# Attention outputs of one pair issued together with the state update and scores of the next, PSUM banks divided anew

## The chip, the cores and the metric

The kernel runs on one core of a Trainium2 chip. The metric is the device time of one execution in microseconds, the median of several runs. A profiled execution shows each engine: TensorE (PE, with its weight loads as PEld), VectorE (DVE), ScalarE (ACT), GpSimd (POOL) and SyncE (SP), which issues the transfers.

## The reference

A linear attention with decay feeds two gated layers over 3072 tokens (B=4, S=768, H=8 heads of D=48; 384 columns).

```python
for t in range(S):
    cur = einsum('bhd,bhe->bhde', u * k[t], v[t])
    y[t] = einsum('bhd,bhde->bhe', r[t], state + cur)
    state = w[t][..., None] * state + einsum('bhd,bhe->bhde', k[t], v[t])
x = y as (3072, 384)
x = ((x @ w_a) * (x @ w_b)) @ w_out          # d_ff 1536
out = square(maximum(x @ w_in, 0)) @ w_out2  # d_ff 2048
```

## The kernel before

**Attention.** The recurrence is taken in chunks of 64 tokens, two chunks at a time: a *pair* p is 128 tokens of one batch for all eight heads, and there are 24 pairs, six to a batch. For a pair, DVE scans the decays (`at_scan`, line 246) and takes reciprocals (`at_recip`, four calls, line 250); POOL scales keys and receptances into the tiles `rk` and `ar` (`at_kr`, `at_rr`) and builds the diagonal term (`at_u1`, `at_diag`). TensorE then has four groups of plain float32 matmuls:

- `at_B` (line 295) transposes the scaled keys into tile `kt`, copied by ACT to `kn` (`at_B2`);
- `at_C` (line 304) makes the state update `ds`, 16 matmuls (8 for the last pair of a batch); DVE adds it to the state `vs` (`at_C2`, four instructions, lines 319 to 323);
- `at_A` (line 281) makes the scores `sc`, 32 small matmuls; DVE copies them under a mask into `ar` (`at_A2`, line 293);
- `at_D` (line 325) makes the outputs `yp`, 32 small matmuls from `ar` and `vs`; ACT copies them to `ys` (`at_D2`), and two transfers store them (`at_store`).

**Layers.** Stage one works in seven blocks of tokens (`BLOCKS1`: 384, 256, 384, then four of 512), stage two in six of 512. Weights come as 64-bit words and are decoded on chip into a high and a low float32r part (`dec_*`, lines 181 to 208: sign, shift, add, high, low, mostly on DVE and ACT); the twelve units of stage one are decoded while the first block runs. A step f of stage one has two products `ua` and `ub` (`prod`, line 350: nine matmuls each into a PSUM tile `pa`), a copy of the first by ACT (line 364), the multiply g on DVE that reads the second (`mult`, line 368), a split of g into `gh` (ACT) and `gl` (POOL), and nine matmuls into three accumulators `acc` (`down`, line 381) some steps later. Stage two has one product a step. The x of a block is loaded from what the attention stored and split by ACT and DVE (`xh`, `xl`).

**PSUM.** There are eight banks: three for `pa` (pool `ps_ab`), three for `acc`, two for the attention's four tiles in turn (pool `ps_at`).

**What sets the order.** Nothing is scheduled on the chip: a planner (class `Plan`, line 47) is run when the program is built. `plan_pair` (line 443) and `plan_step` (line 544) register operations with a cost for each engine, a due time (from the table `KNOB`), what they depend on, and which ring of buffers they take (`acq`) and give back (`rel`). The planner always starts the ready operation with the earliest due time on a free engine, and the order so found is the order in which instructions are issued on each engine. The rings of the plan (line 426) have the numbers of the pools. An engine works strictly in this order: an instruction that waits holds up all behind it.

Of the kernel before, what the change touches and what calls it, by code (L numbers as in the profile page):

```python
# [15 lines left out]
PSUM = bass.MemoryType.PSUM  # L16
DRAM = bass.MemoryType.DRAM

B, H, S, D = 4, 8, 768, 48
NT, DM = B * S, H * D  # L20
F1, F2 = 1536, 2048
C = 64
NP = NT // 128
# [10 lines left out]
EN = HE + HC  # L34
WS = 256.0

KNOB = dict(START=12.39, FIRST=8.84, LEAD=11.15, DEC=4.0, DO=13.13, XO=5.05, X2=-28.46, D2=35.09, LW=13.05, LT=16.03,
            LV=-5.89, LV2=3.32, LN=0.14, scan=2.4, rec=7.4, kr=0.01, rr=-1.74, u1=-0.02, u2=-0.72, dg=-10.16,
            gd=-17.94, A=-4.1, B=9.68, C=-0.57, D=11.41, T2=4.18, EARLY=2.03, WAIT=0)
ENG = dict(kr=("POOL",), da=("DVE", "POOL"), dl=("DVE", "POOL"), rr=("POOL", "DVE"), u2=("DVE",), xs=("DVE",), d2=("ACT",),  # L40
           b2=("ACT",), gl=("POOL",), gh=("ACT",))
SAFE = 2.0 ** 90
FLOOR = 2.0 ** -50
EV, OD = slice(C, C + D), slice(0, D)
# [78 lines left out]
def fused_kernel(ctx, tc, tpk, natpk, vpk, v2pk, upk, cst, w1pk, w2pk, out):  # L123
# [5 lines left out]
    op = ctx.enter_context(tc.tile_pool(name="op", bufs=2))  # L129
    ap = ctx.enter_context(tc.tile_pool(name="ap", bufs=2))  # L130
    dp = ctx.enter_context(tc.tile_pool(name="dp", bufs=1, space=DRAM))
    ps_ab = ctx.enter_context(tc.tile_pool(name="ps_ab", bufs=3, space=PSUM))
    ps_acc = ctx.enter_context(tc.tile_pool(name="ps_acc", bufs=1, space=PSUM))
    ps_at = ctx.enter_context(tc.tile_pool(name="ps_at", bufs=2, space=PSUM))

    ident = const.tile([128, 128], F32, name="ident")
    floor = const.tile([128, HE], F32, name="floor")
# [143 lines left out]
    def at_A(p):  # L281
        t, ar = RK[p], AR[p % 2]
        P = PS[p, "A"] = ps_at.tile([128, HC], F32, tag="at", name="sc")
        for h in range(H):
            ks = slice(TK + h * C, TK + (h + 1) * C)
            cs = slice(h * C, (h + 1) * C)
            nc.tensor.matmul(out=P[0:C, cs], lhsT=t[EV, ks], rhs=ar[EV, 0, cs], start=True, stop=True)  # L287
            nc.tensor.matmul(out=P[C:128, cs], lhsT=t[OD, ks], rhs=ar[OD, 1, cs], start=True, stop=True)
# [36 lines left out]
    def at_D(p):  # L325
        ar, vs = AR[p % 2], VS[p % 2]
        P = PS[p, "D"] = ps_at.tile([112, HC], F32, tag="at", name="yp")
        for h in range(H):
            cs = slice(h * C, (h + 1) * C)
            es = slice(h * D, (h + 1) * D)  # L330
            nc.tensor.matmul(out=P[OD, cs], lhsT=vs[0:112, 0, es], rhs=ar[0:112, 0, cs], start=True, stop=True)  # L331
            nc.tensor.matmul(out=P[EV, cs], lhsT=vs[:, 1, es], rhs=ar[:, 1, cs], start=True, stop=True)  # L332
# [102 lines left out]
    tau = [K["START"]]
# [7 lines left out]
    def plan_pair(p):  # L443
        j, i = place[p]
        m = BLOCKS1[j] // 128
        cold = 1.9 if p <= BLOCKS1[0] // 128 else 1.0
# [5 lines left out]
        def add(name, engs, prio, fn, deps=(), **kw):  # L452
            plan.add((name, p), engs, q - prio, fn, deps, **kw)
# [15 lines left out]
        for k in range(2):  # L469
# [3 lines left out]
            rel=[("nat", p)])  # L473
        add("gd", {"ACT": 1.27}, K["gd"], lambda e: at_guard(p),
            [(("rr", 0), p), (("rr", 1), p), ("A", p), ("B", p), *((("rec", k), p) for k in range(4))], rel=[("rk", p)])
        add("A", {"PE": 1.28 * cold}, K["A"], lambda e: at_A(p), [("kr", p), (("rr", 0), p), (("rr", 1), p)],
            acq=[("at", (p, "A"))])
        add("A2", {"DVE": 1.48}, K["A"], lambda e: at_A2(p), [("A", p), (("dg", 0), p), (("dg", 1), p), "consts"],
            rel=[("at", (p, "A")), ("dg", p)])
        add("B", {"PE": 0.41 * cold}, K["B"], lambda e: at_B(p), [("kr", p), "consts"], acq=[("at", (p, "B"))])  # L480
        add("B2", both(0, 448, *ENG["b2"]), K["B"], lambda e: at_B2(p, e), [("B", p)], acq=[("ky", (p, "k"))],
            rel=[("at", (p, "B"))])
        add("C", {"PE": 1.0 * cold}, K["C"], lambda e: at_C(p), [("B2", p), ("LV2", p), ("D", p - 1)], acq=[("at", (p, "C"))],
            rel=[("ky", (p, "k"))])
        add("C2", {"DVE": 2.35 if p % PPB != PPB - 1 else 1.2}, K["C"], lambda e: at_C2(p), [("C", p), ("C2", p - 1), ("D", p - 1)],
            rel=[("at", (p, "C"))])
        add("D", {"PE": 1.23 * cold}, K["D"], lambda e: at_D(p), [("A2", p), ("C2", p), ("LV", p), ("gd", p)],
            acq=[("at", (p, "D"))], rel=[("ef", p)])
        add(("D2", 0), both(0, HC, *ENG["d2"]), K["D"], lambda e: at_D2(p, 0, e), [("D", p)], acq=[("ky", (p, "y"))])
        add(("D2", 1), both(0, HC, *ENG["d2"]), K["D"], lambda e: (at_D2(p, 1, e), PS.pop((p, "D"))),  # L490
            [("D", p), (("D2", 0), p)], rel=[("at", (p, "D"))])
        for c in range(2):
            add(("ST", c), {"DMA": 0.6}, K["D"], lambda e, c=c: at_store(p, c), [(("D2", c), p), (("ST", c - 1), p)],
                rel=[("ky", (p, "y"))] if c else [], lat=DMA_LAT)
# [118 lines left out]
    for p in range(NP):  # L613
        plan_pair(p)
# [225 lines left out]
```

## Time and profile before

| what | us |
|---|---|
| median of 3 runs | 1009.81 (1009.52 to 1010.01) |
| the profiled execution's own time | 1009.95 |
| its span | 1008.1 |
| TensorE busy in the span | 950.3 (94%) |
| DVE busy | 488.0 (48%) |
| POOL busy | 457.3 (45%) |
| ACT busy | 385.2 (38%) |

The span runs from the first to the last instruction of the program; the execution's own time has 1.85 us more around it. Matmuls overlap in the array, so the time that counts for TensorE is not the length of an instruction but the step from one start to the next.

### The profile page before, as it was taken

The numbers are of one execution on the slowest core, as the hardware profiler recorded it, in microseconds if no ns is written. First come the engines' busy times: TensorE is split into PE (matmuls) and PEld (weight loads), VectorE is DVE, ScalarE is ACT, GpSimd is POOL, SyncE is SP. The second block draws the span as 40 slices with busy tenths as digits, with TensorE's granted clock in tenths as the row PEclk, the third lists the DMA queues.
The fourth block names the chain that finished last, engine by engine and source line by source line (L and its number), as shares of the span: only waits on it lengthen the run. The fifth ranks groups of instructions, "written<-read, shape, count | busy, mean of one in ns | idle before, by whom it ended". The sixth has DMA issues, their size and how long they took to land.

```text
span 1008.1 us, 15015 instructions
## 1 busy us (share of the span) xinstructions
PE 950.3 (94%) x5982; PEld 803.7 (80%) x5982; DVE 488.0 (48%) x585; ACT 385.2 (38%) x591; POOL 457.3 (45%) x359
## 2 busy tenths in 40 slices
PE   3558799999999999999999999999999999999997
PEld 2448699999978787888788888888888888888885
DVE  7799976786564554554222578821121221211111
ACT  1566534333332333233232567433342332422332
POOL 6645478786655455564212254433333233333332
PEclk9969899999999999999999999999999999999999
DMA  9995235544433433332011555010010000100001
GB/s 255 313 315 157 59 96 141 163 121 130 121 86 91 107 106 104 104 92 81 9 40 63 173 196 195 1 53 11 1 64 0 32 32 1 63 1 1 32 0 36
DMA packets 57791, 91.89 MB, mean 91 GB/s; under 512 B 23664, under 2 KB 31600, under 8 KB 57712
## 3 DMA queue, kind: packets, MB, share of 16 engines
q1 hardware_dynamic: 57712, 90.84, 29.7%
q8 instruction: 49, 0.80, 0.3%
q14 instruction: 30, 0.25, 0.1%
HBM read 76.66 MB, written 14.16 MB: 90 GB/s over the span
## 4 chain that ended last, share of the span: by engine, by line
PE 87%; DVE 4%; DMA 3%; issue 2%; ACT 2%; POOL 1%; SPq 0%; DVEq 0%; ACTq 0%; POOLq 0%
PE pa L357 16%; PE pa L358 16%; PE pa L359 15%; PE acc L384 12%; PE acc L386 11%; PE acc L385 11%; PE sc L287 2%; PE yp L331 2%; PE ds L310 2%; DVE z L194 1%; DMA rk<-in_tpk_dram 1%; PE kt L298 1%; DMA vs<-in_vpk_dram 1%; DMA raw<-in_w1pk_dram 1%; DVE raw L190 1%
## 5 line engine op out<-in xcount | busy, mean ns | idle before, releaser
L378 POOL TENSOR_TENSOR gl<-a,gh 128x512 fp32r<-128x512 f32 (+2 forms) x180 | 238.7, 1327 | 445.4 <-ACT gh L175 444.3
L359 PE MATMUL pa<-xh,w 128*128 128x512 f32 (+2 forms) x792 | 295.3, 373 | 5.0 <-DVE w L208 5.0
L358 PE MATMUL pa<-xl,w 128*128 128x512 f32 (+2 forms) x792 | 295.1, 373 | 4.3 <-DVE xl L535 4.3
L357 PE MATMUL pa<-xh,w 128*128 128x512 f32 (+2 forms) x792 | 297.0, 375 | 0.6 <-ACT w L175 0.4
L364 ACT ACTIVATE a<-pa 128x512 f32<-128x512 f32 (+2 forms) x180 | 102.4, 569 | 291.0 <-PE pa L359 239.1
L384 PE MATMUL acc<-gh,w 128*128 128x512 f32 (+2 forms) x540 | 208.7, 386 | 0.0
L386 PE MATMUL acc<-gl,w 128*128 128x512 f32 (+2 forms) x540 | 202.6, 375 | 0.1
L385 PE MATMUL acc<-gh,w 128*128 128x512 f32 (+2 forms) x540 | 202.6, 375 | 0.0
L175 ACT ACTIVATE gh<-a 128x512 fp32r<-128x512 f32 (+2 forms) x180 | 108.3, 602 | 227.2 <-DVE a L368 179.7
L368 DVE TENSOR_TENSOR a<-a 128x512 f32<-128x512 f32 x96 | 67.9, 707 | 253.2 <-ACT a L364 253.2
L359 PEld LDWEIGHTS pa<-xh,w 128*128 128x128 f32 x792 | 150.5, 190 | 29.0 <-DVE w L208 6.2
L358 PEld LDWEIGHTS pa<-xl,w 128*128 128x128 f32 x792 | 150.8, 190 | 27.4 <-DVE xl L535 4.9
L357 PEld LDWEIGHTS pa<-xh,w 128*128 128x128 f32 x792 | 150.6, 190 | 25.1 <-ACT w L175 1.2
L368 DVE TENSOR_TENSOR a<-a,pa 128x512 f32<-128x512 f32 (+2 forms) x84 | 50.8, 606 | 174.9 <-PE pa L359 173.0
L384 PEld LDWEIGHTS acc<-gh,w 128*128 128x128 f32 x540 | 101.5, 188 | 19.7
L386 PEld LDWEIGHTS acc<-gl,w 128*128 128x128 f32 x540 | 101.5, 188 | 17.4 <-POOL gl L378 0.4
L385 PEld LDWEIGHTS acc<-gh,w 128*128 128x128 f32 x540 | 101.6, 188 | 15.3
L252 DVE RECIPROCAL ef<-ef 112x128 f32<-112x128 f32 x96 | 83.3, 916 | 0.4
L277 POOL TENSOR_TENSOR ar<-ident,dg 64x512 f32<-64x512 f32 x48 | 56.1, 1169 | 38.3 <-PE yp L332 23.9
L260 POOL TENSOR_TENSOR ar<-rk,ef 48x512 f32<-48x512 f32 (+1 forms) x48 | 64.7, 1349 | 17.0 <-DVE ef L247 7.4
L247 DVE TENSOR_TENSOR_SCAN ef<-ef,floor 112x520 f32<-112x520 f32 x24 | 38.4, 1603 | 5.0 <-DMA ef<-in_tpk_dram 4.9
L331 PE MATMUL yp<-ar,vs 112*48 112x64 f32 x384 | 30.0, 237 | 10.3 <-issue 9.0
(54 smaller groups left out, 850.6 us busy)
## 6 DMA issues: line engine op xcount, KB each, us to landing
raw<-in_w1pk_dram SPq DMA_DIRECT2D x36, 384.0 KB, 5.7
raw<-in_w2pk_dram SPq DMA_DIRECT2D x32, 384.0 KB, 3.8
rk<-in_tpk_dram SPq DMA_DIRECT2D x24, 448.0 KB, 4.2
v<-in_v2pk_dram SPq DMA_DIRECT2D x24, 384.0 KB, 3.2
nat<-in_natpk_dram SPq DMA_DIRECT2D x24, 384.0 KB, 4.2
ef<-in_tpk_dram SPq DMA_DIRECT2D x24, 227.5 KB, 4.1
vs<-in_vpk_dram SPq DMA_DIRECT2D x48, 96.0 KB, 3.3
xd<-ys SPq DMA_DIRECT2D x48, 96.0 KB, 3.1
```

The source lines that it names most:

```text
L175: nc.scalar.activation(out=out, in_=in_, func=ACTF.Copy, **({} if scale is None else {"scale": scale}))
L252: nc.vector.reciprocal(out=hv(inv(p), C)[:, h0:h0 + 2], in_=hv(ext(p), C + 1)[:, h0:h0 + 2, 1:])
L260: eng(e).tensor_tensor(out=hv(AR[p % 2][rows, c, :], C), in0=hv(RK[p][rows, TR:TK], C), in1=hv(ext(p), C + 1)[rows, :, 0:C], op=ALU.mult)
L357: nc.tensor.matmul(out=out, lhsT=blk(wh, k), rhs=h, start=(k == 0), stop=False)
L358: nc.tensor.matmul(out=out, lhsT=blk(wh, k), rhs=l, start=False, stop=False)
L359: nc.tensor.matmul(out=out, lhsT=blk(wl, k), rhs=h, start=False, stop=(k == KD - 1))
L364: nc.scalar.activation(out=a[:, 0:n], in_=P[:, 0:n], func=func, scale=scale)
L368: eng(e).tensor_tensor(out=a[:, 0:n], in0=a[:, 0:n], in1=b[:, 0:n], op=ALU.mult)
L378: eng(e).tensor_tensor(out=gl[:, 0:n], in0=g[:, 0:n], in1=gh[:, 0:n], op=ALU.subtract)
L384: nc.tensor.matmul(out=o, lhsT=blk(wh, d), rhs=gh[:, 0:n], start=first, stop=False)
L385: nc.tensor.matmul(out=o, lhsT=blk(wl, d), rhs=gh[:, 0:n], start=False, stop=False)
L386: nc.tensor.matmul(out=o, lhsT=blk(wh, d), rhs=gl[:, 0:n], start=False, stop=last)
```

## The change

From the ninth pair on (p >= `ALONE`, which is 8), the outputs of pair p-1, the state update of pair p and its scores are one operation of the planner: `at_D(p - 1)`, `at_C(p)` and `at_A(p)` are issued back to back on TensorE, when all that the three depend on is there. Pair 8 has its update and scores together, and the last pair its outputs alone. The transposes `at_B` stay an operation of their own. The pool `ps_ab` goes from three banks to two and `ps_at` from two to three, and the plan's rings with them. All numbers of `KNOB` but two are new, so that the planner's order changes on every engine, from the start on.

```diff
-KNOB = dict(START=12.39, FIRST=8.84, LEAD=11.15, DEC=4.0, DO=13.13, XO=5.05, X2=-28.46, ...
+KNOB = dict(START=13.52, FIRST=7.12, LEAD=18.8, DEC=4.0, DO=13.32, XO=5.1, X2=-14.73, ...
...
+ALONE = 8
...
-    ps_ab = ctx.enter_context(tc.tile_pool(name="ps_ab", bufs=3, space=PSUM))
+    ps_ab = ctx.enter_context(tc.tile_pool(name="ps_ab", bufs=2, space=PSUM))
...
-    ps_at = ctx.enter_context(tc.tile_pool(name="ps_at", bufs=2, space=PSUM))
+    ps_at = ctx.enter_context(tc.tile_pool(name="ps_at", bufs=3, space=PSUM))
...
-    plan = Plan(dict(ef=3, rk=2, nat=2, dg=2, ky=3, at=2, ab=3, a=3, gg=3, o=2, x=2, z=2), KNOB["WAIT"])
+    plan = Plan(dict(ef=3, rk=2, nat=2, dg=2, ky=3, at=3, ab=2, a=3, gg=3, o=2, x=2, z=2), KNOB["WAIT"])
...
-        add("A", {"PE": 1.28 * cold}, K["A"], lambda e: at_A(p), [("kr", p), (("rr", 0), p), (("rr", 1), p)],
-            acq=[("at", (p, "A"))])
+        alone = p < ALONE
+        depA, acqA = [("kr", p), (("rr", 0), p), (("rr", 1), p)], [("at", (p, "A"))]
+        depC, acqC = [("B2", p), ("LV2", p), ("D", p - 1)], [("at", (p, "C"))]
+        depD, acqD = [("A2", p), ("C2", p), ("LV", p), ("gd", p)], [("at", (p, "D"))]
+        if alone:
+            add("A", {"PE": 1.28 * cold}, K["A"], lambda e: at_A(p), depA, acq=acqA)
+            add("C", {"PE": 1.0 * cold}, K["C"], lambda e: at_C(p), depC, acq=acqC, rel=[("ky", (p, "k"))])
+        elif p == ALONE:
+            add("A", {"PE": 1.9}, K["A"], lambda e: (at_C(p), at_A(p)), [*depA, *depC], acq=[*acqC, *acqA],
+                rel=[("ky", (p, "k"))])
+        else:
+            add("A", {"PE": 2.85}, K["A"], lambda e: (at_D(p - 1), at_C(p), at_A(p)),
+                [*depA, *(x for x in depC if x[0] != "D"), ("A2", p - 1), ("C2", p - 1), ("LV", p - 1), ("gd", p - 1)],
+                acq=[("at", (p - 1, "D")), *acqC, *acqA],
+                rel=[("ky", (p, "k")), ("ef", p - 1)])
...
+        if alone or p == NP - 1:
+            add("D", {"PE": 1.23 * cold}, K["D"], lambda e: at_D(p), depD, acq=acqD, rel=[("ef", p)])
```

TensorE in the steady part, blocks of 512 tokens, before (names of tiles as above; each pair of rows that alternates is shown once):

```order
L386 MATMUL acc_2932<-gl,w_554 128x512
L310 MATMUL ds<-v_93,kn 48x96
L312 MATMUL ds<-v_93,kn 48x96
...
L384 MATMUL acc_2957<-gh,w_554 128x512
...
L359 MATMUL pa<-xh,w_763 128x512
L287 MATMUL sc<-ar_89,rk 64x64
L288 MATMUL sc<-ar_89,rk 64x64
...
L384 MATMUL acc_2932<-gh,w_638 128x512
```

and with the change, at the same place:

```order
L387 MATMUL acc_3702<-gl,w_487 128x512
L332 MATMUL yp<-ar_90,vs_92 48x64
L333 MATMUL yp<-ar_90,vs_92 48x64
...
L311 MATMUL ds<-v_93,kn 48x96
L313 MATMUL ds<-v_93,kn 48x96
...
L288 MATMUL sc<-ar_89,rk 64x64
L289 MATMUL sc<-ar_89,rk 64x64
...
L385 MATMUL acc_3714<-gh,w_487 128x512
```

Update and scores stood apart with acc and pa matmuls between them, and the outputs further on; now outputs (of the other `ar` and `vs` buffer, so of the pair before), update and scores follow each other. After the first block of stage one, TensorE goes from pa or acc matmuls to such groups (kt alone not counted) 52 times before and 23 times now, 15 of them for all three at once.

DVE at the end of the first block, before (L199 and L208 decode weights, L368 is g, L247 the scan, L252 the reciprocals, L293 the masked copy):

```order
L368 TENSOR_TENSOR a<-a,pa 128x384
L199 ISA z<-raw_623,z 128x2304
L293 COPY_PREDICATED ar_89<-mask,sc 64x512 x2
L368 TENSOR_TENSOR a<-a,pa 128x384
L247 SCALAR_TENSOR_TENSOR ef<-ef,floor 112x520
L252 RECIPROCAL ef<-ef 112x128 x4
L273 TENSOR_REDUCE dg<-nat 128x8
L368 TENSOR_TENSOR a<-a,pa 128x384
```

and with the change:

```order
L369 TENSOR_TENSOR a<-a,pa 128x384
L209 TENSOR_TENSOR w_1038<-z,w_1038 128x1152
L200 ISA z<-raw_644,z 128x2304
L369 TENSOR_TENSOR a<-a,pa 128x384
L248 SCALAR_TENSOR_TENSOR ef<-ef,floor 112x520
L209 TENSOR_TENSOR w_1080<-z,w_1080 128x1152
L253 RECIPROCAL ef<-ef 112x128 x4
L369 TENSOR_TENSOR a<-a,pa 128x384 x2
```

The g rows in the first fence are the tenth, eleventh and twelfth of the block; in the second they are the ninth, the tenth, and the eleventh and twelfth together, with the scan and the reciprocals ahead of both.

DVE in the steady part with the change, one pair's time:

```order
L274 TENSOR_REDUCE dg<-nat 128x8
L369 TENSOR_TENSOR a<-a,pa 128x512
L248 SCALAR_TENSOR_TENSOR ef<-ef,floor 112x520
L253 RECIPROCAL ef<-ef 112x128 x4
L369 TENSOR_TENSOR a<-a,pa 128x512 x2
L294 COPY_PREDICATED ar_89<-mask,sc 64x512 x2
L320 TENSOR_TENSOR ds<-ds,vs_91 48x384
```

Before, a g stood between the scan and the reciprocals, and the four state instructions between the first two reciprocals and the last two; now the scan and all four reciprocals stand between one g and the next.

## Rows read from the trace of the kernel before

**Rows 1.** The page: busy time by engine; a DMA issue, with KB and us to landing.

```profile
PE 950.3 (94%) x5982; PEld 803.7 (80%) x5982; DVE 488.0 (48%) x585; ACT 385.2 (38%) x591; POOL 457.3 (45%) x359
...
xd<-ys SPq DMA_DIRECT2D x48, 96.0 KB, 3.1
```

**Rows 2.** Busy time by stretch: start:end, us, engines' busy (x instructions), PE clock, DMA.

```profile
66.40:145.50 79.10, 68.55 (x442) 64.80 (x442) 71.84 (x66) 42.64 (x56) 45.11 (x28) 0.91 0.40 126
145.50:198.00 52.50, 52.49 (x617) 50.25 (x612) 41.23 (x61) 21.01 (x45) 42.33 (x41) 1.00 0.55 154
198.00:517.00 319.00, 318.82 (x2458) 266.01 (x2457) 166.77 (x226) 102.12 (x177) 173.68 (x144) 1.00 0.34 94
```

**Rows 3.** TensorE's waits, 146 us to the end: us in total, times, longest.

```profile
PE yp L332 <- DVE ar L293: 0.2, 1, 0.2
```

**Rows 4.** Instructions in time, TensorE, 322 to 332 us: start us, us, what.

```profile
322.90 0.39 PE L385 MATMUL acc<-gh,w 128*128 128x512 f32 x1
323.12 0.39 PE L386 MATMUL acc<-gl,w 128*128 128x512 f32 x1
323.44 0.28 PE L310 MATMUL ds<-v,kn 128*48 128x96 f32 x1
...
324.24 0.50 PE L384 MATMUL acc<-gh,w 128*128 128x512 f32 x1
324.58 0.40 PE L385 MATMUL acc<-gh,w 128*128 128x512 f32 x1
...
329.58 0.39 PE L359 MATMUL pa<-xh,w 128*128 128x512 f32 x1
329.90 0.27 PE L287 MATMUL sc<-ar,rk 48*64 48x64 f32 x1
...
330.98 0.50 PE L384 MATMUL acc<-gh,w 128*128 128x512 f32 x1
```

**Rows 5.** Instructions in time, TensorE, 205 to 208 us.

```profile
205.40 0.34 PE L359 MATMUL pa<-xh,w 128*128 128x384 f32 x1
205.66 0.28 PE L310 MATMUL ds<-v,kn 128*48 128x96 f32 x1
...
206.46 0.27 PE L287 MATMUL sc<-ar,rk 48*64 48x64 f32 x1
...
207.54 0.45 PE L357 MATMUL pa<-xh,w 128*128 128x384 f32 x1
207.82 0.34 PE L358 MATMUL pa<-xl,w 128*128 128x384 f32 x1
```

**Rows 6.** Instructions in time, DVE, first 150 us; in brackets idle time and releaser.

```profile
32.38 0.58 DVE L319 TENSOR_TENSOR ds<-ds,vs 48x384 f32<-48x384 f32 x1 [5.43 <-PE ds L312]
...
132.20 0.55 DVE L368 TENSOR_TENSOR a<-a,pa 128x384 f32<-128x384 f32 x1 [0.19 <-ACT a L364]
132.67 2.95 DVE L247 TENSOR_TENSOR_SCAN ef<-ef,floor 112x520 f32<-112x520 f32 x1
135.65 3.39 DVE L252 RECIPROCAL ef<-ef 112x128 f32<-112x128 f32 x4
```

**Rows 7.** Groups by line, DVE, 0 to 145.5 us: busy us, mean ns | idle before.

```profile
L252 DVE RECIPROCAL ef<-ef 112x128 f32<-112x128 f32 x24 | 20.4, 908 | 0.1
...
L247 DVE TENSOR_TENSOR_SCAN ef<-ef,floor 112x520 f32<-112x520 f32 x6 | 10.3, 1739 | 2.2 <-DMA ef<-in_tpk_dram 2.2
```

**Rows 8.** Instructions in time, TensorE, 138 to 146 us.

```profile
138.35 0.33 PE L384 MATMUL acc<-gh,w 128*128 128x384 f32 x1
...
142.51 0.55 PE L298 MATMUL kt<-ident,rk 112*128 112x112 f32 x4
143.69 0.86 PE L310 MATMUL ds<-v,kn 128*48 128x96 f32 x8 [0.63 <-ACT kn L175]
...
145.56 0.39 PE L357 MATMUL pa<-xh,w 128*128 128x256 f32 x1
```

**Rows 9.** Instructions in time, DVE, 315 us.

```profile
315.71 0.69 DVE L368 TENSOR_TENSOR a<-a,pa 128x512 f32<-128x512 f32 x1 [4.87 <-PE pa L359]
```

More of the change, by code (lines that the diff above doesn't have):

```diff
@@ L35 @@
 WS = 256.0
-KNOB = dict(START=12.39, FIRST=8.84, LEAD=11.15, DEC=4.0, DO=13.13, XO=5.05, X2=-28.46, D2=35.09, LW=13.05, LT=16.03,
-            LV=-5.89, LV2=3.32, LN=0.14, scan=2.4, rec=7.4, kr=0.01, rr=-1.74, u1=-0.02, u2=-0.72, dg=-10.16,
-            gd=-17.94, A=-4.1, B=9.68, C=-0.57, D=11.41, T2=4.18, EARLY=2.03, WAIT=0)
+KNOB = dict(START=13.52, FIRST=7.12, LEAD=18.8, DEC=4.0, DO=13.32, XO=5.1, X2=-14.73, D2=33.64, LW=15.56, LT=19.97,
+            LV=-2.26, LV2=-0.35, LN=7.51, scan=2.25, rec=6.21, kr=-1.09, rr=5.02, u1=-0.24, u2=2.9, dg=-11.72,
+            gd=-27.44, A=-3.1, B=4.87, C=-16.56, D=10.05, T2=4.14, EARLY=2.77, WAIT=0)
 ENG = dict(kr=("POOL",), da=("DVE", "POOL"), dl=("DVE", "POOL"), rr=("POOL", "DVE"), u2=("DVE",), xs=("DVE",), d2=("ACT",),
            b2=("ACT",), gl=("POOL",), gh=("ACT",))
+ALONE = 8
 SAFE = 2.0 ** 90
@@ L475, in plan_pair @@
             [(("rr", 0), p), (("rr", 1), p), ("A", p), ("B", p), *((("rec", k), p) for k in range(4))], rel=[("rk", p)])
-        add("A", {"PE": 1.28 * cold}, K["A"], lambda e: at_A(p), [("kr", p), (("rr", 0), p), (("rr", 1), p)],
-            acq=[("at", (p, "A"))])
+        alone = p < ALONE
[13 more added lines that the diff above has]
+                rel=[("ky", (p, "k")), ("ef", p - 1)])
+        if not alone:
+            plan.index["C", p] = plan.index["A", p]
+            if p > ALONE:
+                plan.index["D", p - 1] = plan.index["A", p]
+        if alone or p == NP - 1:
+            add("D", {"PE": 1.23 * cold}, K["D"], lambda e: at_D(p), depD, acq=acqD, rel=[("ef", p)])
         add("A2", {"DVE": 1.48}, K["A"], lambda e: at_A2(p), [("A", p), (("dg", 0), p), (("dg", 1), p), "consts"],
@@ L482, in plan_pair @@
             rel=[("at", (p, "B"))])
-        add("C", {"PE": 1.0 * cold}, K["C"], lambda e: at_C(p), [("B2", p), ("LV2", p), ("D", p - 1)], acq=[("at", (p, "C"))],
-            rel=[("ky", (p, "k"))])
         add("C2", {"DVE": 2.35 if p % PPB != PPB - 1 else 1.2}, K["C"], lambda e: at_C2(p), [("C", p), ("C2", p - 1), ("D", p - 1)],
             rel=[("at", (p, "C"))])
-        add("D", {"PE": 1.23 * cold}, K["D"], lambda e: at_D(p), [("A2", p), ("C2", p), ("LV", p), ("gd", p)],
-            acq=[("at", (p, "D"))], rel=[("ef", p)])
         add(("D2", 0), both(0, HC, *ENG["d2"]), K["D"], lambda e: at_D2(p, 0, e), [("D", p)], acq=[("ky", (p, "y"))])
```

## The prediction

> **What bounds the kernel now.** I read the page's busy table first. TensorE is busy for 94% of the span of 1008.1 us; the next engine, VectorE, for 48% [rows 1]. A share over the whole span hides stages, so the second view is the table by stretches [rows 2]. From 66.4 to 145.5 us TensorE works 68.55 of 79.10 us at a granted clock of 0.91, while DVE works 71.84: this stretch is the first block of stage one, and in it DVE, which decodes the weights and runs the attention's vector steps, is the bound. From 145.5 us on TensorE is busy for all of each stretch, at clock 1.00. The third view is the list of TensorE's waits from 146 us to the end: it holds a single wait of 0.2 us [rows 3]. So after 145.5 us only one thing can shorten the kernel: fewer nanoseconds between the starts of TensorE's own instructions.
>
> The fourth view, TensorE's instructions one by one, shows where such nanoseconds are [rows 4]. Products of 512 columns start 0.22 to 0.23 us apart (322.90 to 323.12). The step from the last product to the first ds matmul is 0.32 us (323.12 to 323.44), 0.09 more than a regular one. The ds group takes 0.80 us, and after it the step between the first two products is 0.34 us (324.24 to 324.58), 0.11 too long. The visit of sc begins with the same 0.32 (329.58 to 329.90) and takes 1.08. So each visit to the float32 matmuls of the attention costs about 0.20 us beside its own work: 0.09 on the way in, 0.11 on the way out.
>
> **What the change does, part by part.** *Visits merged.* In the order of before, 52 visits of TensorE to ds, sc or yp stand behind the first block; in the new order there are 23, of which 15 are yp, ds and sc in one piece. That is 29 fewer. The transposes kt stay visits of their own and I count nothing for them. The matmuls themselves are the same in number and shape.
>
> What a junction inside a merged visit costs decides the price. The trace has one pair where sc follows ds directly [rows 5]: ds from 205.66 to 206.46 is 0.80 us and sc from there to 207.54 is 1.08, exactly as when each stands alone [rows 4]; way in and way out are paid once (205.40 to 205.66 is 0.26 against 0.17 for these 384-column products, 207.54 to 207.82 is 0.28). So that junction is free, and each visit saved is worth 0.09 + 0.11 = 0.20: 29 x 0.20 = **5.8 us**. For yp followed by ds at full clock there is no row. Its price lies between nothing and a full way in and out, 0.20; the nearest row is ds followed by sc, so I take nothing. The other end, 15 x 0.20 = 3.0 us, is kept for the range.
>
> The Trainium skill speaks against a free junction: TensorEngine Tiling (Array Packing), Key Properties, says that changing the tiling mode, and not merely the tile, drains TensorE; ds and yp have weights of 128 rows by 48 columns, sc of 48 by 64, so by that page ds to sc is such a change and yp to ds is not. If a drain cost the 0.20 us of a visit, the saving by that rule would be 5.8 - 15 x 0.20 = 2.8 us and the time 1008.1 us by the sum below; the trace's junction of ds and sc does not agree with the rule, so I keep 5.8.
>
> *Later attention outputs.* D of a pair moves into the visit of the pair after it, and with it move its two copies on ACT and its two stores, 3.1 us each to landing [rows 1], and on SP what is queued behind them. Who waits for that is the load of the next block's x. At the closest place, the start of the fourth block, the new order puts 36 products, 39 acc matmuls and a whole visit between the yp of the block's last pair and the block's first product. At 0.17 us each [rows 8] the 75 make 13 us. Store and load by the row of the store take some 6 us; 7 us are left for ACT's and DVE's steps. I cost it at nothing; the cover is that the table issues every pair about 7 us earlier (LEAD), and without it the block's first product would be late by what is missing.
>
> *Banks.* The products lose one of three PSUM banks and the attention gains one. With two, the product ub of a step must wait until DVE's multiply g of the step before has read its bank; with three it was the one before that. DVE is idle before g for 4.87 us in the steady state [rows 9], so g follows ub at once, 0.69 us, and the next ub is more than 2 us later (its own ua stands between, nine products at 0.23). Past the first blocks I cost this at nothing.
>
> *First block.* Here DVE is the bound, so I compare DVE's order. Up to the twelfth and last g both orders hold the same DVE instructions but one reduction, so the end of the block can only move by where they stand. In the new order the scan and the four reciprocals of a pair stand ahead of the eleventh g, not behind it. The scan takes 1.74 us and a reciprocal 0.91 on the mean in this stretch [rows 7], 5.4 us in all; at that very place they took 2.95 + 3.39 = 6.3 [rows 6]. The eleventh g started at 132.20 [rows 6], so it goes to 137.6. The last ub now needs its bank, which comes free 0.5 us later, at 138.1; with its nine products of 0.17 it ends at 139.7, where it ended at 138.35 before [rows 8]. That is 1.3 us late. Behind it stand the same 24 acc matmuls and the visit of a pair, whose ds waited 0.63 us for the copy of kt [rows 8]; now sc and three acc matmuls hide that copy, for one visit more at 0.20: 0.4 back. Sum: **+0.9 us**, by the row at the place itself +1.8.
>
> *Start-up.* The first four pairs are reordered on every engine by the new numbers. What can be won is DVE's largest idle stretch, 5.43 us waiting for ds [rows 6], for which a third attention bank may help; what can be lost is unknown, and I bound it by the same 5.4. In the new order the scan of the fourth pair stands behind a load that is queued on SP behind a store, which waits for ACT, which in turn waits for weights to land; so I expect one such wait in exchange for the other and take 0.
>
> Sum, against the profiled execution's own 1009.95 us (0.14 above the median of the three runs, 1009.81): 1009.95 - 5.8 + 0.9 = **1005.0 us**.
>
> **Rivals.** *A, the two product banks stall TensorE.* After the change DVE's order in a pair's time is g, scan, four reciprocals, g, with no g between them. Scan and reciprocals are 5.4 us; if they start just before ub ends, g is late by that and TensorE waits for the bank by 5.4 + 0.7 less the time to the next ub, which is at the shortest ua and six acc matmuls, 15 x 0.23 = 3.4: 2.7 us in each of 15 pairs, 40 us, 1045 us. It decides from 0.39 us a pair (5.8 / 15). Against it: DVE's 4.87 us of idle before g [rows 9], and that kt and a longer run of acc stand between the two ub in that part of the new order. Chance 0.08. The Trainium skill points this way: Perfetto Trace Analysis, Optimization Strategy, reads the same gap repeated on the engine that should be saturated as a sign of too little SBUF or PSUM for the next tile. No such gap is in the trace of before; whether two banks make one is what this rival asks.
>
> *B, the first 145 us take the gain back.* If the reordered start costs DVE the 5.4 us of the bound, the time is 1010.4; with half of it, 1007.7. For it: DVE is the bound there, and every wait it gets is paid in full. Against it: the set of its work is unchanged. Chance 0.17 for a loss of 2 us and more, of which 0.02 is a loss that makes the kernel slower. The mirror of it, an idle stretch of DVE removed, gives 1000 to 1003; chance 0.13.
>
> *C, the junctions cost what visits cost.* Then the change does not do what it says: 5.8 shrinks to 2.8 (one junction paid) or to nothing (both): 1008.1 to 1010.9. Against it [rows 5]. Chance 0.05.
>
> *The forecast*, 5.8 less and the start within 2 us either way: 1003 to 1007, chance 0.57.
>
> **How the numbers follow.** A measurement of this kernel can tell some 0.2%, 2 us, from no change: 1007.8 to 1011.8. Faster: forecast 0.57, the mirror 0.13, and a third of the 0.15 of B that lies about 1007.7, 0.05: 0.75. Same: the rest of B, 0.10, and C, 0.05: 0.15. Slower: A, 0.08, and B's 0.02: 0.10. The range leaves out A's far end, half of the mirror and the edge of B: 1000.5 to 1009.5.
>
> **What would show it.** Right: in the later stretches TensorE still waits for nothing; yp, ds and sc follow each other with one step of 0.32 before and one of 0.34 behind; the time from the first product of the second block to the end is shorter by 5 to 6 us; the second block starts between 144 and 148.5 us. Wrong in the first term: steps over 0.2 us where yp gives way to ds or ds to sc. Wrong in the bank term: waits of TensorE's products for DVE's multiply past 150 us. Wrong in the start: DVE's idle time before 145 us changed by over 3 us.

## The result and the profile after

The changed kernel takes 998.55 us (median of four runs, 998.08 to 998.79) where the kernel before takes 1009.91 beside it; the ratio is 0.9885, 95% interval 0.9868 to 0.9902. Forecast were 1005.0 us, so 5 us less, in a range of 1000.5 to 1009.5; it became 11.4 us less, below the range. The profiled executions differ by 11.9 us: 1009.95 and 998.08 us, spans 1008.1 and 996.2.

The page after, busy time by engine, answers to [rows 1]. TensorE's matmuls are the same in number.

```profile
PE 940.4 (94%) x5982; PEld 802.0 (81%) x5982; DVE 479.3 (48%) x585; ACT 384.1 (39%) x591; POOL 441.6 (44%) x359
```

The table by stretches of the changed kernel (columns as in [rows 2]) and TensorE's waits from 146 us on, beside [rows 3]:

```profile
66.40:144.30 77.90, 65.78 (x440) 60.30 (x439) 68.55 (x66) 42.49 (x55) 40.02 (x29) 0.95 0.40 125
144.30:198.00 53.70, 53.52 (x655) 51.20 (x655) 45.44 (x63) 22.18 (x47) 44.83 (x43) 1.00 0.54 153
198.00:517.00 319.00, 319.00 (x2458) 273.96 (x2457) 161.35 (x224) 103.10 (x178) 164.39 (x143) 1.00 0.33 94
```

```profile
PE pa L358 <- ACT a L365: 0.2, 1, 0.2
```

TensorE stays the bound from the second block on, and waits for nothing. So the gain lies in the steps between its own starts, as forecast, but with more of it than the steps into and out of a visit. The joined visit in the changed kernel (instructions in time; start us, us, what):

```profile
330.87 0.39 PE L387 MATMUL acc<-gl,w 128*128 128x512 f32 x1
331.19 0.26 PE L332 MATMUL yp<-ar,vs 112*48 112x64 f32 x1
...
332.07 0.22 PE L333 MATMUL yp<-ar,vs 128*48 128x64 f32 x1
332.12 0.25 PE L313 MATMUL ds<-v,kn 128*48 128x96 f32 x1
...
332.70 0.25 PE L311 MATMUL ds<-v,kn 128*48 128x96 f32 x1
332.88 0.27 PE L288 MATMUL sc<-ar,rk 48*64 48x64 f32 x1
...
333.81 0.22 PE L289 MATMUL sc<-ar,rk 48*64 48x64 f32 x1
333.96 0.50 PE L385 MATMUL acc<-gh,w 128*128 128x512 f32 x1
334.30 0.39 PE L386 MATMUL acc<-gh,w 128*128 128x512 f32 x1
```

and a yp alone in the kernel before:

```profile
333.61 0.39 PE L359 MATMUL pa<-xh,w 128*128 128x512 f32 x1
333.93 0.26 PE L331 MATMUL yp<-ar,vs 112*48 112x64 f32 x1
...
334.81 0.22 PE L332 MATMUL yp<-ar,vs 128*48 128x64 f32 x1
334.96 0.50 PE L384 MATMUL acc<-gh,w 128*128 128x512 f32 x1
335.30 0.40 PE L385 MATMUL acc<-gh,w 128*128 128x512 f32 x1
```

Look at the last matmul of each group. Alone, yp's last step is 0.15 us (334.81 to 334.96); before ds it is 0.05 (332.07 to 332.12). The group shrinks from 1.03 to 0.93 us, and ds behind it from 0.80 to 0.76. The last step of ds before sc is 0.18 (332.70 to 332.88), and it is 0.18 too where ds stands alone in the kernel before (324.06 to 324.24 at the place of [rows 4]).

**Where 11.9 us went.** I summed TensorE's steps from the start of the second block's first product to the end of the last acc matmul. Before: 855.6 us (145.56, in [rows 8], to 1001.16); after: 845.0 (144.29 to 989.26). The last acc matmul before, then the two ends of the stretch after:

```profile
1000.77 0.39 PE L386 MATMUL acc<-gl,w 128*128 128x512 f32 x1
```

```profile
144.29 0.28 PE L358 MATMUL pa<-xh,w 128*128 128x256 f32 x1
...
988.88 0.39 PE L387 MATMUL acc<-gl,w 128*128 128x512 f32 x1
```

In the table a regular step is the median one between two products of the same width: 0.12 us for 256 columns, 0.17 for 384, 0.23 for 512.

| part, first product of the second block on | before | after | gained |
|---|---|---|---|
| steps into a visit, over a regular step | 4.84 (69 visits) | 2.00 (38) | 2.84 |
| first steps behind a visit, over a regular step | 7.41 | 3.76 | 3.65 |
| small excess of all other product steps | 1.54 | 0.86 | 0.68 |
| yp groups | 20.10 | 18.11 | 1.99 |
| ds groups | 14.34 | 13.77 | 0.57 |
| sc groups | 19.41 | 19.41 | 0 |
| kt groups, and TensorE's stalls | 5.97 | 6.63 | -0.66 |
| nine acc matmuls now ahead of the second block | 1.56 | 0 | 1.56 |

That is 10.6 us (the expectations below count one or two visits more, those ahead of that product). The other 1.3 us are the first block itself: from its first product (61.42 and 61.46) to the second block's it takes 84.1 us before and 82.8 after. Each is from one execution; in the five kernels below that keep the changed kernel's order up to there, the first block took 82.4 to 82.9.

### The profile page after: what moved, and what is told of

It is laid out like the page before. It is cut to its first block, busy times and chain, and to the rows that moved or that the text cites. A ratio compares the mean times of both kernels' runs of the same rounds, so it can differ in the third digit from the quotient of the medians.

```text
span 996.2 us, 14962 instructions
## 1 busy us (share of the span) xinstructions
PE 940.4 (94%) x5982; PEld 802.0 (81%) x5982; DVE 479.3 (48%) x585; ACT 384.1 (39%) x591; POOL 441.6 (44%) x359
## 4 chain that ended last, share of the span: by engine, by line
PE 88%; DVE 5%; DMA 3%; ACT 1%; issue 1%; SPq 0%; POOL 0%; DVEq 0%; ACTq 0%
PE pa L358 16%; PE pa L360 16%; PE pa L359 16%; PE acc L385 11%; PE acc L387 11%; PE acc L386 11%; PE sc L288 2%; PE yp L332 2%; DVE w L209 1%; DVE z L200 1%; PE kt L299 1%; DMA ef<-in_tpk_dram 1%; PE ds L313 1%; DVE z L195 1%; DMA vs<-in_vpk_dram 1%
## 5 line engine op out<-in xcount | busy, mean ns | idle before, releaser
L379 POOL TENSOR_TENSOR gl<-a,gh 128x512 fp32r<-128x512 f32 (+2 forms) x180 | 235.2, 1308 | 474.4 <-ACT gh L176 469.9
L253 DVE RECIPROCAL ef<-ef 112x128 f32<-112x128 f32 x96 | 82.7, 913 | 0.5
L261 POOL TENSOR_TENSOR ar<-rk,ef 48x512 f32<-48x512 f32 (+1 forms) x48 | 59.0, 1230 | 27.8 <-DVE ef L248 10.0
L294 DVE COPY_PREDICATED ar<-mask,sc 64x512 f32<-64x512 int32 x48 | 35.2, 734 | 39.7 <-PE sc L289 37.7
L278 POOL TENSOR_TENSOR ar<-ident,dg 64x512 f32<-64x512 f32 x48 | 51.5, 1073 | 1.8
L209 DVE TENSOR_TENSOR w<-z,w 128x1152 fp32r<-128x1152 f32 (+1 forms) x22 | 37.2, 1691 | 6.0 <-ACT w L176 6.0
```

The source lines that it names most:

```text
L253: nc.vector.reciprocal(out=hv(inv(p), C)[:, h0:h0 + 2], in_=hv(ext(p), C + 1)[:, h0:h0 + 2, 1:])
L261: eng(e).tensor_tensor(out=hv(AR[p % 2][rows, c, :], C), in0=hv(RK[p][rows, TR:TK], C), in1=hv(ext(p), C + 1)[rows, :, 0:C], op=ALU.mult)
L379: eng(e).tensor_tensor(out=gl[:, 0:n], in0=g[:, 0:n], in1=gh[:, 0:n], op=ALU.subtract)
```

## The experiments

All columns but the median are from the profiled execution; the last one runs from the second block's first product to the last acc matmul. The kernel before, measured beside them, took 1009.5 us (beside yp apart to kt in front), 1010.3 (banks only to kt behind sc), 1009.8 and 1010.2 (the last two pairs of rows).

| kernel | us | first product | first block | behind it |
|---|---|---|---|---|
| before | 1009.9 | 61.4 | 84.1 | 855.6 |
| changed | 998.6 | 61.5 | 82.8 | 845.0 |
| yp apart | 1004.6 | 62.9 | 82.8 | 850.4 |
| yp, sc, ds | 1001.1 | 61.9 | 82.9 | 847.5 |
| before, GpSimd less in three pairs | 1005.2 | 58.5 | 82.0 | 855.4 |
| kt in front | 998.9 | 63.0 | 82.7 | 845.2 |
| banks only | 1012.6 | 58.2 | 89.0 | 855.9 |
| joined, old numbers | 1019.4 | 60.1 | 87.2 | 863.5 |
| new numbers, not joined | 1008.1 | 62.0 | 82.4 | 855.5 |
| kt behind sc | 1011.9 | 62.0 | 82.4 | 857.6 |
| joined from the seventh pair | 1004.9 | 62.7 | 83.4 | 852.4 |
| kt behind sc, from the ninth | 999.9 | 61.8 | 82.9 | 846.3 |
| before, GpSimd less in two pairs | 1006.2 | 60.7 | 81.2 | 855.4 |
| changed, GpSimd less in two pairs | 998.2 | 62.3 | 81.3 | 845.0 |

**The price of a junction.** In the first, yp leaves the joined visit in all 15 places. In 14 it becomes a visit of its own; in one it lands right behind kt, in kt's visit.

```diff
+        if ops[order[k][1]][0][0] in ("dn", "ua", "ub") and all(pos[index[d]] < k for d in need):
+            early.setdefault(k, []).append(p - 1)
...
+            for p in early.get(k, ()):
+                self.at_D(p)
```

> The changed kernel with one thing altered: in 14 of its 15 joined visits yp is issued three acc matmuls (or nine pa matmuls) earlier, as a visit of its own; every other engine keeps its order. Theory T (a visit has four prices: the step into it 0.09 us too long, the last step of its group 0.15 where 0.05 would do, the first step behind it 0.11 too long, a tail of 0.02, and yp to ds pays none of them but 0.04 in ds): 14 x 0.28 = 3.9 us more behind the first block, 1002.0 us, and yp's group back from 0.93 to 1.03 us. Rival R (the prediction's price: 0.20 a visit, a group's own length never changes): 14 x 0.20 = 2.8 us, 1000.9, yp's group 0.93 or 1.03 alike in both kernels. Rival W (what the change gained came from waits and not from the joining): within 0.5 us of 998.1.

Measured: 5.4 us more behind the first block, with yp back at 1.03 us and ds at 0.80 in all 15 places. One of them:

```profile
335.27 0.22 PE L349 MATMUL yp<-ar,vs 128*48 128x64 f32 x1
335.42 0.50 PE L401 MATMUL acc<-gh,w 128*128 128x512 f32 x1
```

Rival W falls, and so does R, the prediction's price of 2.8. T was nearer but had a sign wrong: ds costs 0.04 more, not less, when it doesn't follow yp. It also left out that kt's last step grows from 0.03 to 0.19 where the fifteenth yp follows it. With both put right, T's prices make 14 x (0.09 + 0.11 + 0.02) + 15 x (0.10 + 0.04) + 0.16 = 5.3.

```diff
-lambda e: (at_D(p - 1), at_C(p), at_A(p)),
+lambda e: (at_D(p - 1), at_A(p), at_C(p)),
```

> The changed kernel with the three groups of each joined visit issued as yp, sc, ds in place of yp, ds, sc; number of visits and every other order unchanged. Theory T (the last step of a group costs 0.10 us more wherever the next group cuts the array otherwise; yp and ds cut it alike, sc does not): yp's group goes from 0.93 back to 1.03 us in 15 visits, ds gives back its 0.04: 0.9 to 1.5 us more, 999.0 to 999.6. Rival R (junctions inside a visit are free, whichever they are): 998.1, yp's group 0.93. Rival D (the later ds makes the state, and with it the next outputs, late): a wait of yp or ds of TensorE on DVE behind 150 us, 0.5 us or more in each of 15 visits, 1005 and more.

Measured: 2.5 us more behind the first block, and no wait but the 0.2 us that the changed kernel has, so D falls; with ds's sign put right, T makes 15 x 0.14 = 2.1. The number of visits is that of the changed kernel, so R falls: it is a matter of which group follows. In the trace of this kernel yp's last step before sc is 0.15 again (333.56 to 333.71):

```profile
333.56 0.22 PE L333 MATMUL yp<-ar,vs 128*48 128x64 f32 x1
333.71 0.27 PE L288 MATMUL sc<-ar,rk 48*64 48x64 f32 x1
```

In five of these traces (before, changed, and the kernels yp apart, yp, sc, ds and kt in front) the median last step of a group, by what follows, was the same to a hundredth: yp 0.15 before a product or sc, 0.05 before ds; ds 0.18 before a product or sc; sc 0.15 before a product, yp or ds; kt 0.03 before a product, but 0.19 before sc or yp. The step into a visit is 0.09 too long for yp, ds and sc and 0.00 for kt; the first step behind is 0.10 to 0.11 too long, 0.09 behind kt.

The Trainium skill has the rule for it: TensorEngine Tiling (Array Packing), Key Properties, says that changing the tiling mode, not just the tile, drains TensorE. This trace agrees: yp and ds, both with weights of 48 columns on 112 or 128 rows, join without the extra 0.10, and kt, whose weights have 128 columns like the products', goes in between them with none (0.00 and 0.03). Every other change between these groups pays 0.09 or 0.10, kt before sc or yp 0.16. Which shapes are one mode is read off these steps; no run shows a mode itself.

**The transposes in the visit too.**

```diff
+add("B", {"PE": 0.41}, K["A"], lambda e: at_B(p), [*depA, ..., ("gd", p - 1)], acq=[("at", (p, "B"))], lat=0.0)
+add("A", {"PE": 2.0}, K["A"] + 50, lambda e: (at_A(p), at_D(p - 1)), [("B", p)], ...)
+add("C", {"PE": 0.77}, K["A"] + 50, lambda e: at_C(p), [("A", p), ("B2", p)], acq=acqC, ...)
```

> The changed kernel with the transposes kt in the joined visit too, as kt, sc, yp, ds from the tenth pair on: 15 visits fewer. Theory T: each visit saved is worth 0.09 + 0.11 + 0.02 = 0.22 us beside the last step of its group, and in this order the array is cut anew three times where kt apart and yp, ds, sc cut it anew as often: 15 x 0.22 = 3.3 us less, 994.8. Rival K (ds needs ACT's copy of kt, and the four tiles share three banks, so ds waits in the visit): a wait of ds on ACT of 0.5 us or more in most of the 15 visits takes the gain back: 998 to 1005. Rival R2 (a visit of kt is cheap already, since the way out of it is paid only by float32 matmuls with small weights): within 1 us of 998.1.

Measured: 845.2 behind the first block against 845.0, R2's case; ds never waits, so K falls. Steps into visits and behind them gave 2.7 us (15 visits fewer), but kt's last step, 0.03 before a product, became 0.19 before sc, which took 2.4 back, and stalls 0.65. In its trace kt x4 from 332.38 to 332.86 takes 0.48 us where it takes 0.32 alone:

```profile
332.38 0.55 PE L299 MATMUL kt<-ident,rk 112*128 112x112 f32 x4
332.86 0.27 PE L288 MATMUL sc<-ar,rk 48*64 48x64 f32 x1
```

With kt behind sc instead that price should not arise. This was tried twice, from the seventh pair and from the ninth on. In both, a pair's loads, scan, reciprocals and scaled keys are also due 10 us sooner (`AHEAD`), so the order changes on the other engines too.

```diff
+plan.add(("D", p - 1), {"PE": 0.95}, q - K["A"], lambda e: at_D(p - 1), [..., ("kr", p + 1)], ...)
+add("A", {"PE": 1.87}, K["A"] + 50, lambda e: (at_C(p), at_A(p)), [("D", p - 1)], ...)
+add("B", ..., K["B"] if p <= ALONE + 1 else K["A"] + 20 + AHEAD, lambda e: at_B(p),
+    [("kr", p), "consts", *([("A", p - 1)] if p > ALONE + 1 else [])], acq=[("at", (p, "B"))])
```

> The changed kernel with the joining from the seventh pair on, and the transposes kt of the next pair issued right behind sc where they are ready (15 of 18 times): 24 visits behind the first block where the changed kernel has 40. Theory T (with kt in front, as tried, sc pays 0.16 for the new cut of the array; behind sc it pays nothing that sc did not pay already, and its own 0.09 step out replaces sc's 0.11): 15 x 0.13 = 1.9 us, five fewer small-weight visits at 0.22 = 1.1, three more yp to ds at 0.14 = 0.4: 3.4 us less from the second block's start to the last acc matmul than the changed kernel's 845.0, 995 in all. Rival K (kt takes the bank of yp, which ACT has to copy first, and needs DVE and GpSimd a pair ahead): waits of kt, or of pa, of 3 us and more in all, 998 and more.

> As the kernel with kt behind sc, but joined from the ninth pair on as in the changed kernel, so that the place where kt waited 8.9 us for ACT (at the start of the third block) is ordered as in the changed kernel; 12 of 15 kt stand right behind sc. Theory T: 12 x 0.13 = 1.6 us less than the changed kernel's 845.0 behind the first block, 997 in all. Rival K (kt in the bank of yp waits for ACT's copies at each block's start): a wait of kt of over 2 us, and behind it steps of TensorE at half its clock, 1000 or more.

The first fell to rival K: one wait of 8.9 us. In the trace ACT waits, in issue order, for a store that frees the tile o and then for the load of x that is queued behind it; its copy of yp, whose bank kt needs, is issued behind both (ACT, instructions in time, then TensorE's waits):

```profile
200.19 0.39 ACT L177 ACTIVATE o<-acc 128x256 f32<-128x256 f32 x1 [5.31 <-DMA x1d<-o]
205.41 1.16 ACT L177 ACTIVATE xh<-xl 128x1152 fp32r<-128x1152 f32 x1 [4.84 <-DMA xl<-xd]
206.48 1.19 ACT L177 ACTIVATE ys<-yp 48x512 f32<-48x512 f32 x2
```

```profile
PE kt L300 <- ACT ys L177: 8.9, 1, 8.9
```

The second has no such wait. The steps into and behind visits are 0.7 us less than in the changed kernel, but TensorE's stalls take 1.1 more, kt's groups 0.6, and one late kt behind sc 0.4: 846.3, no gain, and 999.9 us in all. T's 1.6 us did not come, and K's wait of kt did not either.

```diff
-ALONE = 8
+ALONE = 5
```

> The changed kernel with the joining from the seventh pair on (ALONE 5): 20 visits of small-weight matmuls behind the first block where the changed kernel has 25, 18 junctions of yp and ds where it has 15, and 18 visits of kt alone where it has 15. Theory T by the prices measured so far: 5 x 0.22 + 3 x 0.14 less 3 x 0.09 = 1.2 us less behind the first block, 843.7 from the second block's start to the last acc matmul, 997.4 in all. Rival S (the joined operation of the early pairs has to wait, since DVE is busiest there): waits of yp, ds or sc between 140 and 200 us of 1.2 us and more, 998.5 or more.

Measured: 852.4 behind the first block and 1004.9 us in all (the profiled execution was the slowest of six, 1002.6 to 1007.1). The time is in S's range, but S's reason is not in the trace: yp and sc wait for nothing and ds for 0.2 us. From 199 us on kt waits for GpSimd's scaled keys, and later products wait for DVE. The two longest waits:

```profile
PE kt L299 <- POOL rk L257: 3.7, 1, 3.7
PE pa L358 <- DVE a L369: 1.3, 1, 1.3
```

None of the versions tried beats the changed kernel.

**Banks, numbers, joining.** Three runs put the parts in one by one: the banks alone, the banks and the joining with the old `KNOB`, and the new `KNOB` and banks with nothing joined (`ALONE = 24`).

> The kernel before with the banks alone redivided (two for the products, three for the attention), the old numbers kept and nothing joined. Theory T (the banks bring nothing by themselves, all behind the first block is the price of visits): 70 visits as before, from the second block's start to the last acc matmul 855.1 to 856.1 us where before has 855.6, in all 1008.5 to 1011. Rival A1 (two product banks stall TensorE): waits of pa on DVE or ACT behind 150 us, 3 us and more. Rival A2 (a third attention bank is what frees the start): second block 3 us sooner or more, 1006.5 or less.

> The kernel before with the banks redivided and the groups joined as in the change, but with the old numbers. 38 visits behind the first block (15 of them kt alone) where before has 70 (17 kt alone). Theory T: 30 fewer visits of small-weight matmuls at 0.09 + 0.11 + 0.02 = 0.22 us, 15 last steps of yp shorter by 0.10 and as many ds by 0.04, two visits of kt at 0.09: 6.6 + 2.1 + 0.2 = 8.9 us less from the second block's start to the last acc matmul, 846.7; the first block as before (84.1 us); 1000.6 in all. Rival N (without new numbers the joined operation waits for the latest of its inputs and TensorE with it): waits of yp, ds or sc behind 150 us of 3 us and more in all, 1003.5 or more.

> The changed kernel with its numbers and banks, but with nothing joined: 69 visits behind the first block, 15 of kt alone. Theory T (the new numbers give the shorter first block, the joining the rest): first block 82.6 to 83.0 us long as in the changed kernel where before has 84.1, from the second block's start to the last acc matmul 853 to 856, in all 1006 to 1008.5. Rival F (what was won in the first block came from the joining, or from a chance of that one execution): first block 84 us or longer, 1009 to 1011. Rival N2 (the numbers are what brings the gain behind the first block): 848 or less from the second block's start to the last acc matmul, below 1002 in all.

The banks alone: 855.9 behind the first block, T; the only wait of a product on another engine is 0.2 us, so A1 falls. A2 falls too: the first product does come 3.2 us sooner, but the first block is 4.8 us longer, so that the whole, 1012.6, lies above T's 1011. The new numbers without joining: 855.5 behind the first block and 1008.1 in all, as T had it, and a first block of 82.4, 0.2 below T's range. So with these numbers the joining is worth 855.5 - 845.0 = 10.5 us, of which 1.6 are stalls that the kernel without it has, and the numbers and banks together give the shorter first block. The new numbers with the old banks were not run. With the old numbers the joined kernel is 9 us slower than before (ratio 1.0094, 1.0074 to 1.0115). The time is in N's range, but the joined groups hardly wait: 0.7 us, not 3. What waits is kt, for GpSimd's scaled keys, and the first products of a block, for x. Its waits of over 0.2 us behind 146 us:

```profile
PE kt L299 <- POOL rk L257: 4.7, 1, 4.7
PE pa L358 <- ACT xh L176: 4.4, 1, 4.4
PE pa L359 <- DVE xl L551: 1.0, 1, 1.0
PE yp L333 <- DVE ar L294: 0.7, 2, 0.5
```

and what follows the second and third, at the start of a block (instructions in time, then busy time by stretch, columns as in [rows 2]):

```profile
455.33 0.40 PE L387 MATMUL acc<-gl,w 128*128 128x512 f32 x1
460.16 0.79 PE L358 MATMUL pa<-xh,w 128*128 128x512 f32 x1 [4.43 <-ACT xh L176]
461.95 0.79 PE L359 MATMUL pa<-xl,w 128*128 128x512 f32 x1 [1.00 <-DVE xl L551]
462.54 0.63 PE L360 MATMUL pa<-xh,w 128*128 128x512 f32 x1
462.97 0.63 PE L358 MATMUL pa<-xh,w 128*128 128x512 f32 x1
```

```profile
455.00:465.00 10.00, 4.57 (x11) 3.01 (x11) 9.77 (x12) 2.56 (x3) 5.42 (x4) 0.74 0.79 251
465.00:475.00 10.00, 10.00 (x110) 8.14 (x110) 7.00 (x11) 4.50 (x8) 4.60 (x4) 0.92 0.19 41
```

A wait costs more than itself: having waited 4.4 and 1.0 us, TensorE starts products 0.43 us apart where 0.23 is regular, which is 512 columns at the lower of its two levels, 1.2 GHz; the granted clock of the two stretches is 0.74 and 0.92.

**The first block.** DVE's instructions there differ in length from one place to another. In the kernel before (DVE, then GpSimd, in time) the shift of the decode (L194) takes 1.35 us, and 2.17 where GpSimd's split of g ran beside it. The sign (L190) takes 0.75 us, and 1.85 beside GpSimd's scaling of the keys:

```profile
85.07 2.17 DVE L194 SCALAR_TENSOR_TENSOR z<-z,raw 128x1152 int32<-128x1152 int32 x1
87.16 0.75 DVE L190 TENSOR_SCALAR raw<-raw 128x1152 int32<-128x1152 int32 x1
...
89.10 1.35 DVE L194 SCALAR_TENSOR_TENSOR z<-z,raw 128x1152 int32<-128x1152 int32 x1
...
94.19 1.85 DVE L190 TENSOR_SCALAR raw<-raw 128x1152 int32<-128x1152 int32 x1
```

```profile
84.19 1.83 POOL L378 TENSOR_TENSOR gl<-a,gh 128x384 fp32r<-128x384 f32 x1 [0.27 <-ACT gh L175]
...
93.01 2.41 POOL L256 TENSOR_TENSOR rk<-rk,ef 112x512 f32<-112x512 f32 x1
```

Against the shortest of its line, DVE's instructions of the first block are 13.8 us too long in the kernel before, 13.4 of it in those beside GpSimd work; after, about 12. Reciprocals, which read one tile, don't change (0.91 us on the mean in both). The sign reads one tile as well and does change, so two tiles are not the condition. What the extra is, the rows tell: up to the second block, 18 instructions of the decode and the scan are over 0.2 us too long in the kernel before, and beside each a GpSimd instruction that had begun earlier was still running. Each is longer by the rest of that instruction less 0.12 to 0.15 us (the shift at 85.07: GpSimd's ends at 86.02, 0.95 later, and the extra is 0.82). In the changed kernel the same holds for all 14. So DVE waits inside its instruction until GpSimd's is done; one sign, at 38.64, did not. Three runs took GpSimd work away to test it.

```diff
 def at_u1(p, i, e="POOL"):
+    if 3 <= p <= 5:
+        return
...
 def at_diag(p, c, e="POOL"):
+    if 3 <= p <= 5:
+        return
```

> The kernel before with one thing left out: GpSimd's multiplies for the diagonal term and its diagonal tiles (nat and ar, lines 269 and 277) of the fourth to sixth pair, so that the outputs of these pairs are not the reference's. Issue order of all that stays is unchanged. Theory P (a vector instruction that reads two tiles is held up while GpSimd runs beside it; those beside lines 269 and 277 between 94 and 145 us were 0.3 to 1.1 us longer than the same instruction elsewhere, 7.6 us together, some of it beside other GpSimd work too): the second block of stage one starts 3 to 7 us sooner, at 138.5 to 142.5, sign, shift and add of the decode come back to 0.75 and 1.35 us where they stood beside these lines, and the time is 1003 to 1007. Rival Q (the end of the first block is set by where the vector instructions stand and by waits, their lengths vary for other reasons): second block between 144.5 and 146.5, 1009 to 1011.

The second block started at 140.46 and the time was 1005.2, both where P had them. The lengths came back only in part: some of the decode's steps were at 0.75 and 1.35 us again, others now ran beside other GpSimd work and stayed long (the low part, L208, took 2.34 beside `at_rr`). And 2.9 of the 5.1 us came before the first product, so the test was repeated without the work of the fourth pair (`4 <= p <= 5`), in both kernels.

> The kernel before without GpSimd's multiplies for the diagonal term and its diagonal tiles of the fifth and sixth pair alone (the outputs of these pairs are then not the reference's), so that the start up to the first product, which the run without those of the fourth pair shortened by 2.9 us, stays as it is. Beside the eight instructions left out stood 7.6 us of lengthened vector instructions, 4.1 of them beside nothing else of GpSimd. Theory P (the lengthened instructions set the length of the first block): first block 80 to 82.5 us long where before has 84.1, its start at 60.5 to 62.5, 1005.5 to 1009. Rival Q (the 2.2 us that the first block lost in that run followed from its earlier start): first block 83.5 us or longer, 1009 to 1011.

> The changed kernel without the same eight GpSimd instructions of the fifth and sixth pair (the outputs of these pairs are then not the reference's). Beside them stood 2.8 us of vector instructions longer than elsewhere. Theory P (the lengthened vector instructions still set the length of the first block): 80 to 81.3 us where the changed kernel and four kernels with the same first block have 82.4 to 82.9. Rival L (something else ends the first block now; among those kernels the time in lengthened instructions went from 9.0 to 11.8 us at one and the same length): 82 to 82.9. Behind the first block nothing changes, 845 us; 996 to 999.5 in all.

The first block took 81.2 us in the first, 2.9 less, P; DVE did the same work in 3.5 us less. Busy time by stretch, the first block of the kernel before and of that run:

```profile
61.40:145.50 84.10, 69.25 (x444) 65.09 (x443) 76.84 (x72) 47.51 (x61) 45.11 (x28) 0.89 0.43 132
```

```profile
60.70:142.00 81.30, 67.62 (x445) 62.87 (x444) 73.29 (x73) 47.94 (x61) 33.76 (x21) 0.93 0.47 144
```

In the second it took 81.3, at P's edge, 1.5 less for about 3 us of lengthening removed. So in the kernel before, with DVE the bound, GpSimd's work beside it costs time in the first block: DVE's busy time fell by 3.5 us and the block by 2.9. In the changed kernel's order the sum of the lengthening does not set the length: it went from 9.0 to 11.8 us among kernels whose first block took 82.4 to 82.9, and the run that took 81.3 has 9.0 as well. What GpSimd's own shorter work gave (45.1 to 33.8 us in the kernel before) was not separated in either, and what ends that block now stays open.

## Why the prediction was wrong, point by point

**The visits saved.** Right in count and price. 29 visits of small-weight matmuls went, and two of kt alone that I hadn't counted; steps into and out of them gave 2.84 + 3.65 = 6.5 us, 0.21 a visit. The 0.7 over 5.8 was spent on kt and stalls. A small excess in the steps further behind gave 0.7 more, which 0.20 left out.

**The junction of yp and ds is the step that failed.** Forecast were 4.9 us less and the profiled executions show 11.9. Of the 7 us between, 3.3 are in the term of the visits, the rest in the first block. "Its price lies between nothing and a full way in and out" put no gain below nothing, and no reason excluded one. A group carries a price inside its own length, the long last step, and where yp and ds join it is not paid: 15 x 0.14 = 2.1 us. With the 0.7 of small excess and 0.5 us of one yp that had been held up (its wait is in [rows 3]), this makes the 3.3 us by which the term of 5.8 came out at 9.1.

**The reading of [rows 5] failed with it.** That ds takes 0.80 "exactly as when each stands alone" was taken to show a free junction. It shows that ds pays its long last step in both places. The Trainium skill's rule on the drain was set aside on this row. The runs agree with it, and the sum by it was wrong only because I priced a drain as a whole visit. That rule, applied to the end of each group, would have pointed to yp before ds.

**The first block.** Forecast +0.9, found -1.3, and nine acc matmuls moved ahead of its end besides, 1.6, for which the sum had no term. The step that failed is "The last ub now needs its bank, which comes free 0.5 us later, at 138.1". DVE in the changed kernel at the place in question, then TensorE:

```profile
129.30 0.54 DVE L369 TENSOR_TENSOR a<-a,pa 128x384 f32<-128x384 f32 x1
129.77 1.23 DVE L248 TENSOR_TENSOR_SCAN ef<-ef,floor 112x520 f32<-112x520 f32 x1
...
135.47 0.49 DVE L369 TENSOR_TENSOR a<-a,pa 128x384 f32<-128x384 f32 x1
137.72 0.55 DVE L369 TENSOR_TENSOR a<-a,pa 128x384 f32<-128x384 f32 x1 [1.76 <-PE pa L360]
```

```profile
135.60 0.45 PE L387 MATMUL acc<-gl,w 128*128 128x384 f32 x1
135.89 0.34 PE L358 MATMUL pa<-xh,w 128*128 128x384 f32 x1
```

The eleventh g did go behind scan and reciprocals, but the last ub did not wait for it: ub starts at 135.89, and that g ends at 135.96. In six other kernels with this order ub starts 0.07 or 0.08 us before the end of that g too. So ub ended 0.9 us sooner than before (the acc matmul behind it starts at 137.45, before at 138.35) and not 1.3 later. The 0.4 behind ub came as forecast: from there to the second block it is 6.84 us where it was 7.21. Which release of a bank ub waited for, if any, was not separated.

The time of that g was off as well, 135.47 and not 137.6. The forecast added 5.4 us to its old start. But in the new order the add and the two masked copies, 2.9 us, no longer stand between the tenth g and the eleventh, and a low part of 1.3 does. The scan starts at 129.77 where it started at 132.67, and it takes 1.23 us, not the mean of 1.74 or the 2.95 of [rows 6]. The scan of 2.95 had GpSimd at work beside it:

```profile
131.87 2.66 POOL L208 TENSOR_TENSOR w<-z,w 128x1152 fp32r<-128x1152 f32 x1 [9.36 <-ACT w L175]
```

So one instruction is not equally long in both orders, which "the end of the block can only move by where they stand" took for granted. The Trainium skill, SBUF — State Buffer, Who interferes with whom, says that a vector instruction with two SBUF inputs contends with a GpSimd instruction that reads SBUF, and that whichever comes second waits. The scan and the shift here agree, with 1.23 and 2.95, 1.35 and 2.17 us, where GpSimd had started first.

**What held.** The banks cost nothing behind the first block: TensorE's one wait there is 0.2 us. In the first block, which that term left out, the banks alone cost 4.8 us with the old numbers. Rivals A and C fell, and B's loss did not come. B's mirror did not either: DVE was idle for 23.1 us before the second block where it had been for 20.5. The start-up stayed where it was (61.42, 61.46), in part by luck: in the other kernels with the same order ahead of the first product it came between 61.8 and 63.0. The loads behind later stores were costed at nothing, with the larger LEAD as the cover; with the old numbers a block's first product waited 4.4 us for x, as the text said it would. And the second block started at 144.29, at the lower end of the 144 to 148.5 named.

## What to carry to other kernels

Price a stretch of small matmuls from its neighbours on both sides: the step in, the last step of the group, the first steps behind. Then ask which groups cut the array alike, and put those next to each other; joining groups that differ saves less than the count of visits says. And where VectorE is the bound, a list of its instructions is not its time: look at what GpSimd does beside each, and take the undisturbed length from the shortest row of its line. Then test whether that lengthening lies on the path: here it did in one order and not in the other.

## What the runs showed that I had not expected

Transposes in float32, with weights of 112 rows by 128 columns, go in between products almost free (0.00 in, 0.03 last step, 0.09 behind), but cost 0.19 where a group with small weights follows. After a wait of 8.9 us, in the kernel with kt behind sc, products of 384 columns started 0.32 us apart where 0.17 is regular, for 5 us (208.9 to 213.7): half speed, as after the 4.4 and 1.0 us shown above. And a program's first product came between 61.5 and 63.0 us with one and the same order ahead of it, while the first block behind it took 82.4 to 82.9, and 83.4 in one kernel whose block ends in another order.
